# Attention, ELU-MoE and SoLU-MoE: a planned opening, v in halves, and four weight fetches moved behind the last stores

## The chip, the cores and the metric

One core of one Trainium2 chip runs the whole program once. The metric is device time in microseconds. Engines are TensorE (PE; PEld is its weight load), VectorE (DVE), ScalarE (ACT), GpSimd (POOL) and SyncE (SP), which issues the DMAs.

## What is computed

Three blocks in a row, on 4608 tokens of 512 features. Inputs are fp32; the weights come to the chip as 64-bit words.

```
k_p, v_p = k, v averaged over groups of 8 positions            # 576 -> 72
a = exp(s - max s),  s = q k_p^T / 8;  a = a / (sum a + 1e-9)
x = a v_p                                                       # 8 batches x 8 heads
h = x w_in;  g = h if h > 0 else exp(h) - 1;  x = g w_out       # 512 -> 2048 -> 512
h = x w2_in; e = exp(h - max h);  u = h * e / (sum e + 1e-9)    # 512 -> 1024
y = ((u - mean u) / sqrt(var u + 1e-6) * g_ln) w2_out           # -> 512
```

## The kernel before

**Work and stages.** Attention is cut into 32 units: 8 batches of NP = 4 head pairs. A unit loads k, q and v (`att_load`), sums k and v over groups of 8 (`att_kr`, `att_vr`), scales the sums (`att_kc` by 1/64, `att_vc` by 1/8, both on ACT), multiplies q with k (`att_scores`), takes maximum, exponential and normaliser (`att_max`, `att_exp`, `att_soft`), transposes on PE (`att_T`), multiplies with v (`att_V`) and splits the result into a high and a low fp32r part, `xh` and `xl` (`att_x`). Every large product is three products of such parts: high by high, low by high, high by low.

The ELU-MoE goes over blocks of 512 tokens. The first three blocks are done plainly, an h tile at a time (`h` L893, `o` L948). The other six go as three pairs, by a scheme of seven products instead of eight (`h_step` L1088, `mul_o` L1178). Attention units of later blocks are laid between. Weights are converted on chip from the 64-bit words (`conv`, L685 to L695: ACT, then DVE) and split into parts (`conv_split`, L709 and L710: ACT, then POOL).

The SoLU-MoE follows, again with seven products, over pairs n of token tiles. Product by product it writes the banks X, Y and Z (`z_mul`, PE L1285): P1 writes X, P2 writes Y, S2 adds onto X, and so on. ACT copies X to an `sn` tile after P1 and after S2 (`snap`, L1295), before the next product may add to it. From X, Y, Z and the copies come two tiles, `ha` and `hb`. Each goes through maximum, `e` (L1342), product with the normaliser (DVE L1348), subtraction of the mean (ACT L1353) and squares (L1358). Then the tile is turned: a few on PE (`pt`, L1404, copied by ACT L1410), the others by DVE in 32x32 squares (L1372), stored to memory (`zd`, L1377), loaded again (`dT`, four DMAs, L1384) and split by ACT (`dhl<-dT`, L1392) and DVE. The last product is `po` (L1423), 24 matmuls; ACT scales it into `ot` (L1429), which is stored.

**Who sets the order.** Each engine runs its instructions in program order. Three things set it.

- The opening (loads and `startup()`, L1466 to L1612) stands inside `tc.manual_schedule()` and runs as written. `busy(n, tag)` there puts n small matmuls without use on PE, in five calls of 6, 3, 8, 4 and 7. Being fp32, each of them shows as two rows in the trace and as one in the listings of order below.
- What is recorded up to the end of the ELU-MoE is ordered by `settle` (L31 to L270): it lists the instructions with assumed costs and due times, runs through them in assumed time and takes on each engine what is ready and most urgent.
- The SoLU-MoE is ordered by `arrange` (from about L1825). Each step is an entry `op(key, eng, dur, deps, f, ..., lat, at)`: its engine, assumed duration, what it waits for, and an assumed latency behind it. PE's order is fixed by the list `seq`; the other engines' order follows from assumed times.

Before the SoLU-MoE its weights are brought in by `fetch` (L799). The last four, `(0, 0)` to `(1, 1)`, are the parts of w2_out (`w<-o2d`, 1 MB each), which `po` needs. They are called at the end of the last pair, ahead of `p2_load(1)` (`x1r<-x1d`, L1228) and of the last two stores `x1d<-xo` (`o_done`, L1192). `arrange` knows nothing of them:

```python
deps = [("lo2", n)] + ([("st", outs[j - 2])] if j > 1 else [])
op(k, "PE", 5.46, deps + [before], z_out, n)
...
op(("hi2", i), "ACT", 1.0, [("l", i)] + free3, t_hi, i)
op(("p1", n), "ACT", 0.56, [("P1", n), ("ha0", n - 1)], snap, n, "p1", "X")
```

`hi2` is the row `dhl<-dT`, `("l", i)` its load, `p1` the first `sn` copy of pair n.

Of the kernel before, what the change touches and what calls it, by code (L numbers as in the profile page):

```python
# [22 lines left out]
class Step:  # L23
    def __init__(self, eng, idx, key):
        self.eng, self.idx, self.key = eng, idx, key
        self.ins, self.acc, self.deps, self.tiles, self.turn = [], [], set(), [], set()
        self.dur = self.lat = 0.0
        self.bytes = 0


def settle(tc, nc, stacks, PEND=2.6, WINDOW=10):  # L31
    GAP, RATE, LOOK = 0.06, 350e3, 0.35
# [32 lines left out]
    def cost(op, i, ins, outs):  # L65
# [9 lines left out]
        n = max(cols(o) for o in ins + outs)  # L75
        if op.eng == "SP":
            op.dur += 0.37
            op.bytes += max(o.ap[0][1] * cols(o) * size(o) for o in (ins[0], outs[0]))
        elif op.eng == "DVE":
            op.dur, op.lat = max(0.18, 0.068 + n * (0.0013 if str(outs[0].dtype).endswith("uint32") else 0.00109)), 0.09  # L80
        elif op.eng == "Activation":
            op.dur, op.lat = max(0.28, (0.057 if type(i).__name__ == "InstActivation" else 0.026) + n * 0.00096), 0.1
        else:
            op.dur, op.lat = 0.1 + n * 0.003, 0.1

    ops, fixed = [], 0
    for i in list(nc.cur_bb.bb.instructions):
# [5 lines left out]
        eng = str(i.engine).split(".")[-1]  # L93
        ins, outs = ([o for o in x if hasattr(o, "bass_ap")] for x in (i.ins, i.outs))
        fi, fo = [foot(o) for o in ins], [foot(o) for o in outs]
        key = fo[0][0] if fo else None
        if not (eng == "PE" and ops and ops[-1].eng == "PE" and ops[-1].key == key and len(ops[-1].ins) < 12):
            ops.append(Step(eng, len(ops), key))
        op = ops[-1]
        op.ins.append(i)  # L100
# [91 lines left out]
    for o in ops:  # L192
        if o.eng == "PE":
            want[o] = t
            t += o.dur
    latest = {}
    for o in reversed(topo):
        lat = PEND + 0.1 + o.bytes / RATE if o.eng == "SP" else o.lat
# [4 lines left out]
    manual = {e: [o for o in ops[:fixed] if o.eng == e] for e in engines}  # L203
    chain = [o for o in ops[fixed:] if o.eng == "PE"]
    ready = {e: {} for e in engines + (None,)}
    for o in ops:
        if not left[o]:
            ready[o.eng][o] = 0.0
    free, done, begun, order = dict.fromkeys(engines, 0.0), {}, {}, {e: [] for e in engines}
    lag = pipe = 0.0  # L210
    for _ in ops:
        best = min(((x, None, o) for o, x in ready[None].items()), key=lambda x: x[0], default=None)
        for e in engines if best is None else ():
            r, f = ready[e], free[e]
            if not r:
                continue
            if manual[e]:
                k = manual[e][0]
                if k not in r:
                    continue  # L220
            elif e == "PE":
                chain = [o for o in chain if o not in done] if chain and chain[0] in done else chain
                near = [o for o in chain[:3 * WINDOW] if o not in done][:WINDOW]
                near = [o for o in near if o in r]
                if not near:
                    continue
                first = min(max(f, r[o]) for o in near)
                k = next(o for o in near if max(f, r[o]) <= first + 0.02)
            else:
                first = min(max(f, x) for x in r.values())  # L230
                k = min((o for o in r if r[o] <= first + LOOK), key=lambda o: latest[o] + 3.0 * max(0.0, r[o] - first))
                for q in r if e in ("Activation", "DVE") else ():
                    end = max(f, r[k]) + k.dur
                    if q is not k and r[q] < end:
                        mine = max(0.0, end - latest[q] - lag)
                        other = max(0.0, max(f, r[q]) + q.dur - latest[k] - lag)
                        if other < mine - 0.05:
                            k = q
            begin = max(f, r[k])
            if best is None or begin < best[0]:  # L240
                best = begin, e, k
        begin, e, k = best
        if e == "PE":
            lag = max(lag, begin - want[k])
        begun[k] = begin
        if e is not None:
            free[e] = begin + k.dur
        if e is None:
            done[k] = begin
        elif e == "SP":  # L250
            pipe = max(free[e] + PEND - 0.8, pipe) + k.bytes / RATE
            done[k] = pipe + 0.9
        else:
            done[k] = free[e] + k.lat
        if e is not None:
            order[e].append(k)
            if manual[e]:
                manual[e].pop(0)
        del ready[e][k]
        for q in after[k]:  # L260
            left[q] -= 1
            if not left[q]:
                ready[q.eng][q] = max(
                    [done[d] + (0 if d.eng == q.eng == "PE" else GAP) for d in q.deps] + [begun[d] for d in q.turn]
                )
# [8 lines left out]
def kernel(  # L274
# [68 lines left out]
    NTREE = 3  # L343

# [13 lines left out]
    def att_load(i, what="kqv"):  # L358
        b, p = units[i]
        if i < NP:  # L360
            if ("kq", p) not in st:
# [3 lines left out]
                n = P * POOL  # L365
                v_t = st["v2"][0:SK, (p % 2) * n:(p % 2 + 1) * n].rearrange("s (c t) -> s c t", t=POOL)
                st["kq", p] = (kq[:, 0:S], kq[:, S:2 * S], v_t)
            k_t, q_t, v_t = st["kq", p]
        else:
            k_t = pa.tile([P, S], F32, name=f"k{i}", tag="k", bufs=1)  # L370
            v_t = pa.tile([SK, P, POOL], F32, name=f"v{i}", tag="v", bufs=1)
# [8 lines left out]
        if "v" in what:  # L380
            nc.sync.dma_start(out=v_t, in_=v[b, p].rearrange("s h d t -> s (h d) t"))

    def pool_tree(dst, src):
        n = POOL // 2
        while n > 1:
            nc.gpsimd.tensor_tensor(src[:, :, 0:n], src[:, :, 0:n], src[:, :, n:2 * n], op=ALU.add)
            n //= 2
        nc.gpsimd.tensor_tensor(dst, src[:, :, 0], src[:, :, 1], op=ALU.add)
# [25 lines left out]
    def att_kc(i):  # L414
        kp, kr = att_kv(i)[0], st.pop(("kr", i))
        nc.scalar.mul(kp[0:64, 0:SK], kr[0:64, :], 1.0 / (8 * POOL))
        nc.scalar.mul(kp[64:128, SK:2 * SK], kr[64:128, :], 1.0 / (8 * POOL))

    def att_vr(i):
        v_t = st["kq", units[i][1]][2] if i < NP else st["ld", i][1]  # L420
        vr = st["vr", i] = pa.tile([SK, P], F32, name=f"vr{i}", tag="vr")
        if i < NTREE:
            pool_tree(vr, v_t)
        else:
            nc.vector.tensor_reduce(vr, v_t, axis=AX, op=ALU.add)

    def att_vc(i):
        nc.scalar.mul(att_kv(i)[1], st.pop(("vr", i)), 1.0 / POOL)

    def att_setup(i):  # L430
        for part in (att_kr, att_kc, att_vr, att_vc):
            part(i)
# [50 lines left out]
    def att_soft(i):  # L483
# [82 lines left out]
    def rest(part):  # L566
# [15 lines left out]
        elif part == 1:  # L582
# [3 lines left out]
            nc.vector.tensor_scalar(sm, sm, 1e-9, None, op0=ALU.add)  # L586
# [68 lines left out]
    def conv_load(key):  # L655
# [1386 lines left out]
```

## Time and profile before

| what | value |
|---|---|
| median of 3 runs | 1245.41 us (1244.01 to 1245.87) |
| the profiled execution | 1244.96 us |
| its span in the profile | 1243.2 us, so 1.76 us lie around it |
| mean granted clock of TensorE | 0.998 |
| PE, DVE, ACT, POOL busy | 99%, 80%, 67%, 14% |
| chain that ended last | PE 95%, DVE 3%, DMA 1% |
| DMA | 263.31 MB, mean 212 GB/s |

The span runs from the first instruction to the last. A busy share is an average over stages of different kinds: the opening, in which PE waits for loads and for DVE, and the rest, where PE streams. A timeline row gives start, duration, engine, line and operation, and in brackets how long the engine had been idle before it and what ended that. Matmul rows overlap; 512-column matmuls of one stream start 0.23 us apart.

### The profile page before, as it was taken

The page shows a single profiled execution, that of the slowest core. Times are in us where ns is not written, and L with a number is a line of the kernel's source. Part 1 is how long each engine was busy: PE and PEld are TensorE (multiplying, and loading weights), DVE is VectorE, ACT ScalarE, POOL GpSimd, SP SyncE. Part 2 cuts the span into 40 slices and gives each one's busy share as a digit, 9 for nine tenths or more (in the row PEclk, how much of TensorE's full clock was granted, in tenths as well). Part 3 has the DMA queues.
Part 4 walks back from the last instruction along what each step waited for, and adds up shares of the span by engine and source line. Part 5 has one row for each costly group of instructions (what it writes and reads, how often), then busy time and mean ns, then how long its engine had stood idle before and what let it go on. Part 6 is the DMA issues. An engine that isn't in the chain of part 4 may idle for free.

```text
span 1243.2 us, 17288 instructions
## 1 busy us (share of the span) xinstructions
PE 1229.9 (99%) x5768; PEld 993.1 (80%) x5768; DVE 995.0 (80%) x1484; ACT 827.1 (67%) x1405; POOL 170.4 (14%) x148
## 2 busy tenths in 40 slices
PE   7999999999999999999999999999999999999998
PEld 6777787777787878788888788888888888888887
DVE  8898999898677789875788587997788787878763
ACT  7789666666657785557774477753676776767664
POOL 4645222332210011000000000000000000000000
PEclk9999999999999999999999999999999999999999
DMA  9598667677456867796667888788545544554341
GB/s 317 171 283 260 215 223 245 223 263 262 142 177 209 249 211 237 223 309 200 205 202 223 280 272 272 248 264 323 208 156 170 161 131 158 167 156 144 110 151 53
DMA packets 177065, 263.31 MB, mean 212 GB/s; under 512 B 16464, under 2 KB 96848, under 8 KB 175952
## 3 DMA queue, kind: packets, MB, share of 16 engines
q1 hardware_dynamic: 176976, 262.21, 65.6%
q8 instruction: 46, 0.75, 0.2%
q14 instruction: 43, 0.35, 0.1%
HBM read 182.46 MB, written 79.69 MB: 211 GB/s over the span
## 4 chain that ended last, share of the span: by engine, by line
PE 95%; DVE 3%; DMA 1%; issue 1%; ACT 0%; SPq 0%; ACTq 0%; DVEq 0%
PE po L1423 16%; PE hA L1088 16%; PE oA L1178 16%; PE o L948 10%; PE h L893 10%; PE zX L1285 8%; PE zZ L1285 4%; PE at L446 3%; PE oB L1178 3%; PE hB L1088 3%; PE at L531 3%; PE zY L1285 2%; PE pt L505 2%; PE pr L510 0%; DVE es L495 0%
## 5 line engine op out<-in xcount | busy, mean ns | idle before, releaser
L1423 PE MATMUL po<-w,dhl 128*128 128x512 f32 x864 | 203.7, 392 | 0.0
L1178 PE MATMUL oA<-op,wr 128*128 128x512 f32 x864 | 202.3, 392 | 0.0
L1178 PEld LDWEIGHTS oA<-op,wr 128*128 128x128 f32 x864 | 160.9, 188 | 37.6 <-issue 2.2
L1423 PEld LDWEIGHTS po<-w,dhl 128*128 128x128 f32 x864 | 162.1, 188 | 35.2
L1168 ACT CAST op<-g 128x1024 fp32r<-128x1024 f32 x84 | 87.7, 1052 | 59.7 <-PE oA L1178 34.8
L1169 DVE TENSOR_TENSOR op<-g,op 128x1024 fp32r<-128x1024 f32 x84 | 102.7, 1230 | 21.0 <-ACT op L1168 20.3
L1088 PE MATMUL hA<-sS,wr 128*128 128x512 f32 x414 | 104.0, 393 | 0.1
L1285 PE MATMUL zX<-w,xh 128*128 128x512 f32 x288 | 100.8, 392 | 0.0
L1363 POOL TENSOR_TENSOR sc<-sc,mhalf 128x1 f32<-128x1 f32 x36 | 20.9, 585 | 559.2 <-DVE sc L1362 295.3
L814 POOL TENSOR_TENSOR wol<-wo,woh 128x512 fp32r<-128x512 f32 x48 | 70.0, 1458 | 161.8 <-ACT woh L813 161.7
L1088 PEld LDWEIGHTS hA<-sS,wr 128*128 128x128 f32 x414 | 76.8, 188 | 18.7 <-issue 1.4
L495 POOL TENSOR_TENSOR es<-es,sm 128x720 f32<-128x720 f32 x28 | 43.5, 1552 | 312.2 <-DVE sm L493 228.8
L893 PE MATMUL h<-xh,wh 128*128 128x512 f32 x192 | 78.3, 408 | 1.4 <-DVE e L910 1.4
L948 PE MATMUL o<-gh,woh 128*128 128x512 f32 x192 | 78.2, 407 | 0.0
L893 PE MATMUL h<-xh,wl 128*128 128x512 f32 x192 | 75.2, 392 | 0.0
L893 PE MATMUL h<-xl,wh 128*128 128x512 f32 x192 | 75.2, 391 | 0.0
L948 PE MATMUL o<-gh,wol 128*128 128x512 f32 x192 | 75.0, 391 | 0.0
L1100 ACT COPY sp<-hA 128x512 f32<-128x512 f32 x72 | 42.3, 588 | 40.3 <-PE hA L1088 39.3
L1108 DVE SCALAR_TENSOR_TENSOR g<-ep,g 128x512 f32<-128x512 f32 x72 | 50.5, 703 | 20.9 <-ACT ep L1107 20.6
L1285 PEld LDWEIGHTS zX<-w,xh 128*128 128x128 f32 x288 | 54.1, 188 | 12.3
L1295 ACT COPY sn<-zX 128x512 f32<-128x512 f32 x54 | 31.8, 588 | 47.2 <-PE zX L1285 47.0
L1162 DVE TENSOR_TENSOR g<-g,g 128x1024 f32<-128x1024 f32 x48 | 61.0, 1288 | 0.1
(366 smaller groups left out, 2755.0 us busy)
## 6 DMA issues: line engine op xcount, KB each, us to landing
wr<-w3d SPq DMA_DIRECT2D x168, 256.0 KB, 2.8
wr<-w1d SPq DMA_DIRECT2D x161, 256.0 KB, 3.1
raw<-in_w SPq DMA_DIRECT2D x48, 512.0 KB, 6.8
dT<-zd SPq DMA_DIRECT2D x128, 128.0 KB, 2.7
v<-in_v SPq DMA_DIRECT2D x32, 288.0 KB
x1r<-x1d SPq DMA_DIRECT2D x9, 1024.0 KB, 5.9
out<-ot SPq DMA_DIRECT2D x36, 256.0 KB, 3.0
w1d<-ci SPq DMA_DIRECT2D x16, 512.0 KB, 3.3
```

The source lines that it names most:

```text
L495: eng.tensor_tensor(es, es, bc(sm, n), op=ALU.mult)
L814: nc.gpsimd.tensor_tensor(ol, t[:, f % 4, :], oh.bitcast(F32), op=ALU.subtract)
L893: nc.tensor.matmul(h[:, 0:n], a[g][:, kk, fo:fo + P], x[j][:, kk, 0:n], start=(kk == 0 and m == 0), stop=(kk == KDM - 1 and m == 2), skip_ ...
L948: nc.tensor.matmul(acc, a[:, dm * P:(dm + 1) * P], x[:, 0:n], start=(f == 0 and m == 0), stop=(f == NF - 1 and m == 2))
L1088: nc.tensor.matmul(bank, w[:, a, kk], x[:, b, kk], start=(start and m == 0), stop=(stop and m == 5), skip_group_check=True,)
L1108: gate["dve"] = nc.vector.scalar_tensor_tensor(d, e, 1.0, h, op0=ALU.subtract, op1=ALU.max).ins
L1162: nc.vector.tensor_tensor(d, x, y, op=op)
L1168: gate["act"] = nc.scalar.copy(o[:, 0], src).ins
L1169: gate["dve"] = nc.vector.tensor_tensor(o[:, 1], src, o[:, 0].bitcast(F32), op=ALU.subtract).ins
L1178: nc.tensor.matmul(banks[d], ws[i][:, a, d * P:(d + 1) * P], o[:, b, i], start=(start and t == 0 and i == 0 and m == 0), stop=(stop and t ...
L1285: nc.tensor.matmul(bank, x[:, o:o + P], w[:, y + k, :], start=(start and m == 0), stop=(stop and m == 5), skip_group_check=True,)
L1423: nc.tensor.matmul(po, a[:, c], b[c // 4][:, c % 4, :], start=(m == 0), stop=(m == 3 * NC2 - 1))
```

## The change

It does eight things.

1. `settle` gets other assumed costs: issue times of SP, a model of 16 DMA pipes by packet size, a port that DVE and POOL share. It treats each `busy` matmul as a step of its own that it puts where it expects PE to be idle.
2. The opening is no longer manual: `settle` orders it, the first loads excepted. `busy(56, "B")` is one call of 56 instead of 28 in five.
3. k's scaling in units 1 to 3 (`KPOOL`), and the normaliser product in units 2 and 3 (`NPOOL`), go to POOL.
4. v is laid out as two halves of 64 columns; `att_vc` is gone, and its 1/8 is folded into the normaliser, which is multiplied by 8.
5. The 64-bit words of w_in come as one 1 MB transfer, not as two of 512 KB. The first two conversions work in halves, through a PSUM tile `cu`.
6. The loads of i4, o4, i6, unit 4 and the rest move from ahead of `startup()` into it.
7. For the last pair, the first o product is split in two and stands between the last h products (`o_step`).
8. The four fetches move out of the last pair into `arrange`, as SP steps that form a chain; each `po` waits for the last of them. So they come behind the last `x1d<-xo` stores.

```diff
+    def idle(key):
+        return key is not None and key.startswith("busy")
...
+                    if fill is not None and at(fill) + (0.28 if f > 6.0 else 0.55) < first:
+                        k = fill
+                        k.dur = 0.26 if f > 6.0 else 0.52
...
     def att_kc(i):
         kp, kr = att_kv(i)[0], st.pop(("kr", i))
+        if i in KPOOL:
+            nc.gpsimd.tensor_scalar(kp[0:64, 0:SK], kr[0:64, :], 1.0 / (8 * POOL), None, op0=ALU.mult)
+            nc.gpsimd.tensor_scalar(kp[64:128, SK:2 * SK], kr[64:128, :], 1.0 / (8 * POOL), None, op0=ALU.mult)
+            return
...
-    def att_vc(i):
-        nc.scalar.mul(att_kv(i)[1], st.pop(("vr", i)), 1.0 / POOL)
...
-        nc.vector.tensor_scalar(sm, sm, 1e-9, None, op0=ALU.add)
+        nc.vector.tensor_scalar(sm, sm, 1e-9, float(POOL), op0=ALU.add, op1=ALU.mult)
         nc.vector.reciprocal(sm, sm)
-        eng = nc.vector if i < NP else nc.gpsimd
+        eng = nc.vector if i < NP and i not in NPOOL else nc.gpsimd
...
-        for a in range(2):
-            c, d = i + a, raw[:, a, :]
-            if kind == "i":
-                nc.sync.dma_start(
-                    out=d.rearrange("p (k f) -> p k f", k=KDM),
-                    in_=w_in[:, c * P:(c + 1) * P].rearrange("(k p) f -> p k f", p=P),
-                )
...
+        if kind == "i":
+            nc.sync.dma_start(
+                out=raw.rearrange("p a f -> p (a f)").rearrange("p (k f) -> p k f", k=KDM),
+                in_=w_in[:, i * P:(i + 2) * P].rearrange("(k p) f -> p k f", p=P),
+            )
...
+        busy(56, "B")
         att_kr(0)
         att_kc(0)
-        busy(6, "B")
         S_(0)
...
-    with tc.manual_schedule():
+    with ExitStack():
         for i in range(NP):
             att_load(i, "kq")
...
             if last and s == 6:
-                for n in ((0, 0), (0, 1), (1, 0), (1, 1)):
-                    fetch(n)
                 p2_load(1)
                 with loose(gate["x1r"]):
                     o_done(c, s)
...
     op("x1", None, 0.0, [], at=17.0)
+    for m, n in enumerate(((0, 0), (0, 1), (1, 0), (1, 1))):
+        op(("o2", n), "SP", 0.5, [("o2", p) for p in ((0, 0), (0, 1), (1, 0))[max(m - 1, 0):m]], fetch, n, lat=9.0)
...
-            deps = [("lo2", n)] + ([("st", outs[j - 2])] if j > 1 else [])
+            deps = [("lo2", n), ("o2", (1, 1))] + ([("st", outs[j - 2])] if j > 1 else [])
             op(k, "PE", 5.46, deps + [before], z_out, n)
```

**How instructions move: PE in the opening.** Around the last attention product ahead of the first h tile (`at<-a,kz`, the fourth of its kind), before:

```order
L531 MATMUL at_341<-a_288,kz 64x512 x2
L1493 MATMUL busy<-ident 128x128 x4
L505 MATMUL pt_0_356<-ident,es_265 72x128 x4
L505 MATMUL pt_1_362<-ident,es_265 72x128 x4
L531 MATMUL at_368<-a_312,kz 64x512 x2
L1493 MATMUL busy<-ident 128x128 x7
L531 MATMUL at_384<-a_355,kz 64x512 x2
L893 MATMUL h_398<-xh_325,wh 128x512
```

and with the change:

```order
L559 MATMUL pt_1_339<-ident,es_226 72x128 x4
L1561 MATMUL busy<-ident 128x128 x8
L585 MATMUL at_379<-a_310,kz 64x512 x2
L559 MATMUL pt_0_387<-ident,es_284 72x128 x4
L559 MATMUL pt_1_393<-ident,es_284 72x128 x4
L585 MATMUL at_399<-a_332,kz 64x512 x2
L1561 MATMUL busy<-ident 128x128
L585 MATMUL at_406<-a_386,kz 64x512 x2
L1561 MATMUL busy<-ident 128x128
L961 MATMUL h_420<-xh_128,wh 128x512
```

Of the seven fills ahead of the last product one is left there, one stands behind it, and eight stand ahead of the second product, where four stood. Further on, six fills stand ahead of the fourth slice of the first h tile and seven ahead of the second tile.

**ACT at the first `po`.** Pair 2 begins behind the first `po`. `sn<-zX` are its copies, `dhl<-pt` belongs to a tile turned on PE, `dhl<-dT` to one turned through memory. Before:

```order
L1295 COPY sn<-zX 128x512
L1353 ACTIVATE e_8696<-e_8696,sc 128x1024
L1295 COPY sn<-zX 128x512
L1410 CAST dhl<-pt_8735 128x512
L1410 CAST dhl<-pt_8740 128x512
L1358 ACTIVATE sq,sc<-e_8689 128x1024
L1295 COPY sn<-zX 128x512
L1342 ACTIVATE e_8805,sc<-ha,sc 128x1024
L1429 ACTIVATE ot<-po,sc 128x512
L1358 ACTIVATE sq,sc<-e_8696 128x1024
L1353 ACTIVATE e_8805<-e_8805,sc 128x1024
L1392 CAST dhl<-dT 128x1024
```

and with the change:

```order
L1426 ACTIVATE sq,sc<-e_8623 128x1024
L1426 ACTIVATE sq,sc<-e_8630 128x1024
L1330 CAST xh_8615<-x1r_8449 128x512
L1330 CAST xh_8615<-x1r_8449 128x256
L1330 CAST xh_8615<-xs_8659 128x1024
L1460 CAST dhl<-dT 128x1024
L1497 ACTIVATE ot<-po,sc 128x512
L1363 COPY sn<-zX 128x512 x2
L1478 CAST dhl<-pt_8734 128x512
L1478 CAST dhl<-pt_8739 128x512
L1410 ACTIVATE e_8756,sc<-ha,sc 128x1024
L1363 COPY sn<-zX 128x512
```

`dhl<-dT` and the first `ot` have moved from behind three `sn` copies to ahead of the first two of them. PE's order at this place is the same in both: `po`, then P1 (zX), P2 (zY) and S2 (zX) of pair 2.

**SP at the end of the last pair**, before:

```order
L1192 DMA x1d<-xo 128x512 x2
L806 DMA w_8488<-o2d 128x2048
L806 DMA w_8490<-o2d 128x2048
L806 DMA w_8492<-o2d 128x2048
L806 DMA w_8494<-o2d 128x2048
L1228 DMA x1r_8496<-x1d 128x4x512
L1192 DMA x1d<-xo 128x512 x2
L1228 DMA x1r_8683<-x1d 128x4x512
L1377 DMA zd_81<-hb 128x4x256
```

and with the change:

```order
L1260 DMA x1d<-xo 128x512 x2
L1296 DMA x1r_8449<-x1d 128x4x512
L1260 DMA x1d<-xo 128x512 x2
L874 DMA w_8471<-o2d 128x2048
L874 DMA w_8531<-o2d 128x2048
L874 DMA w_8609<-o2d 128x2048
L1296 DMA x1r_8617<-x1d 128x4x512
L874 DMA w_8647<-o2d 128x2048
L1445 DMA zd_81<-hb 128x4x256
L1452 DMA dT<-zd_81 32x4x256 x4
```

The four `w<-o2d` have moved behind the last two `x1d<-xo` and the first `x1r`, and the last of them behind the second `x1r`.

## Rows read from the trace of the kernel before

**Rows 1.** The page: each engine's busy time, share of the span, instructions.
```profile
PE 1229.9 (99%) x5768; PEld 993.1 (80%) x5768; DVE 995.0 (80%) x1484; ACT 827.1 (67%) x1405; POOL 170.4 (14%) x148
```

**Rows 2.** Waits of PE, whole program: waiter, releaser, us, times, longest.
```profile
PE pt L505 <- DVE es L495: 2.9, 2, 1.9
...
PE rs L572 <- PE at L446: 0.7, 1, 0.7
...
PE at L531 <- ACT kz L428: 0.2, 1, 0.2
```

**Rows 3.** Timeline of PE, 0 to 40: start us, us, instruction, [idle before].
```profile
11.39 1.95 PE L1493 MATMUL busy<-ident 128*128 128x128 f32 x16
...
27.70 3.07 PE L1493 MATMUL busy<-ident 128*128 128x128 f32 x14
30.70 1.08 PE L531 MATMUL at<-a,kz 72*64 72x512 f32 x4
...
38.84 0.50 PE L893 MATMUL h<-xh,wh 128*128 128x512 f32 x1 [1.39 <-DVE e L910]
```

**Rows 4.** Timeline of ACT, 10 to 40.
```profile
28.59 0.31 ACT L428 ACTIVATE kz<-vr 72x128 f32<-72x128 f32 x1
```

**Rows 5.** Stretches: busy us per engine (x count), granted clock, DMA share, GB/s.
```profile
10.00:24.00 14.00, 11.02 (x78) 7.89 (x76) 13.10 (x24) 13.91 (x50) 9.42 (x10) 1.00 1.06 332
28.00:32.00 4.00, 4.00 (x19) 3.07 (x19) 3.97 (x5) 2.65 (x7) 1.21 (x1) 0.71 1.07 347
860.00:884.00 24.00, 24.00 (x110) 19.70 (x109) 13.23 (x21) 10.86 (x19) 0.00 (x0) 1.00 0.97 375
884.00:1239.00 355.00, 355.00 (x1562) 290.82 (x1560) 269.59 (x476) 240.00 (x362) 20.86 (x36) 1.00 0.44 139
```

**Rows 6.** Timeline of PE, 876 to 912.
```profile
884.15 5.66 PE L1423 MATMUL po<-w,dhl 128*128 128x512 f32 x24
...
892.43 0.39 PE L1285 MATMUL zX<-w,xh 128*128 128x512 f32 x1
```

**Rows 7.** Timeline of ACT, 876 to 906.
```profile
891.24 0.59 ACT L1295 COPY sn<-zX 128x512 f32<-128x512 f32 x1 [1.04 <-PE zX L1285]
891.72 1.15 ACT L1353 ACTIVATE e<-e,sc 128x1024 f32<-128x1024 f32 x1
...
899.30 0.68 ACT L1429 ACTIVATE ot<-po,sc 128x512 f32<-128x512 f32 x1
...
902.40 1.04 ACT L1392 CAST dhl<-dT 128x1024 fp32r<-128x1024 f32 x1
```

**Rows 8.** Instructions of L495: count, ns min/median/max, first and last start us.
```profile
L495 POOL TENSOR_TENSOR es<-es,sm x28: 1392/1394/2450, 59.1 to 646.3; 128x720 f32<-128x720 f32 x28
...
L495 DVE TENSOR_TENSOR es<-es,sm x4: 808/1274/1814, 13.3 to 23.4; 128x576 f32<-128x576 f32 x4
```

**Rows 9.** Timeline of SP, 855 to 912: DMA issues.
```profile
861.78 3.14 SPq L806 DMA_DIRECT2D w<-o2d  x4
...
876.29 0.53 SPq L1228 DMA_DIRECT2D x1r<-x1d  x1
894.58 0.38 SPq L1377 DMA_DIRECT2D zd<-hb  x1
897.50 1.76 SPq L1384 DMA_DIRECT2D dT<-zd  x4
```

**Rows 10.** Timeline of DVE, 876 to 912.
```profile
883.61 1.22 DVE L1336 TENSOR_REDUCE sc<-hb 128x1 f32<-128x1024 f32 x1 [0.44 <-ACT hb L1326]
...
889.30 1.28 DVE L1348 SCALAR_TENSOR_TENSOR e<-e,sc,hb 128x1024 f32<-128x1024 f32 x1
...
890.70 1.22 DVE L1266 TENSOR_TENSOR xl<-xs,xh 128x1024 fp32r<-128x1024 f32 x1
...
893.31 1.24 DVE L1372 STREAM_TRANSPOSE hb<-e 128x1024 f32<-128x1024 f32 x1
```

**Rows 11.** The tile dT: landing times of its loads.
```profile
DMA to landing us min/median/max: 2.2/2.7/4.0
```

More of the change, by code (lines that the diff above doesn't have):

```diff
@@ L27, in __init__, with settle @@
         self.dur = self.lat = 0.0
-        self.bytes = 0
-def settle(tc, nc, stacks, PEND=2.6, WINDOW=10):
-    GAP, RATE, LOOK = 0.06, 350e3, 0.35
+        self.bytes = self.move = self.wide = 0
+        self.port = False
+def settle(tc, nc, stacks, PEND=2.6, FAST=1.7, WINDOW=10):
+    GAP, LOOK = 0.06, 0.35
     masks = {}
@@ L194, in settle @@
             want[o] = t
-            t += o.dur
+            t += o.dur * (not idle(o.key))
     latest = {}
     for o in reversed(topo):
-        lat = PEND + 0.1 + o.bytes / RATE if o.eng == "SP" else o.lat
+        lat = PEND + 0.1 + o.move if o.eng == "SP" else o.lat
         lat += o.dur + (GAP if o.eng not in ("PE", None) else 0)
@@ L202, in settle @@
     engines = ("PE", "Activation", "DVE", "Pool", "SP")
[L203 to L219, printed above, removed]
-                    continue
[L221 to L228, printed above, removed]
-            else:
[L230 to L264, printed above, removed]
-                )
@@ L266, in settle @@
+    order, begun, done = forward(latest)
     info = mybir.DependencyInfo(mybir.DependencyClass.NoSync, mybir.DependencyReason.DATA)
@@ L380, in att_load @@
         if "v" in what:
[L381 removed]
+            nc.sync.dma_start(out=v_t, in_=v[b, p])
     def pool_tree(dst, src):
@@ L683, in conv @@
         wcv[key] = w2
+        if key in (("i",0),("o",0)):
+            for a in range(2):
+                c = slice(512 * a, 512 * a + 512)
+                u = ps.tile([P, 512], F32, name="cu", tag="A", bufs=4)
+                t = u.bitcast(U32)
+                nc.scalar.activation(u, hw.bitcast(F32)[:, c], AF.Abs, scale=2.0**-112)
+                nc.scalar.activation(lw[:, c], raw.bitcast(U8)[:, 3::8][:, c], AF.Identity, scale=1.0 / 32, bias=b31)
+                if a:
+                    yield
+                nc.vector.scalar_tensor_tensor(t, t, 3, lw[:, c], op0=ALU.logical_shift_left, op1=ALU.bitwise_or)
+                nc.vector.scalar_tensor_tensor(
+                    wu[:, c], hw[:, c], 0x80000000, t, op0=ALU.bitwise_and, op1=ALU.bitwise_or
+                )
+            yield
+            return
         nc.scalar.activation(w, hw.bitcast(F32), AF.Abs, scale=2.0**-112)
@@ L1509, in startup @@
         att_kc(2)
-        busy(3, "B")
         S_(2)
@@ L1518, in startup @@
         att_kc(3)
-        busy(8, "B")
         T(0)
@@ L1538, in startup @@
         att_x(0)
+        for key in (("i", 4), ("o", 4), ("i", 6)):
+            conv_load(key)
+        att_load(NP)
+        rest_load()
         att_vr(3)
@@ L1752, with o_step @@
         count = 0
+        def o_step(s, t, ds=(0, 1)):
+            nonlocal step, credit
+            if t == ds[0] == 0:
+                ox["b"] = o_banks(s, "CBA" if last else "ABA")
+            banks = ox["b"]
+            mul_o(s, t, banks, s in (0, 1, 2), s in (1, 5, 6), ds)
+            if ds[-1] == 0:
+                return
+            if s + 1 < 7:
+                for i in range(2):
+                    w_ring(("o", s + 1, 2 * t + i))
+                n = ORDER[s + 1]
+                if n in ("S2", "S3"):
+                    g_sum(n, t)
+                if n == "S4":
+                    with loose(gate["dve"]):
+                        g_sum(n, t)
+                with loose(gate["keep"]) if last and s == 4 else ExitStack():
+                    g_op(s + 1, t)
+            elif not last:
+                for m in (2 * t, 2 * t + 1):
+                    if m < 7:
+                        w_ring(("i", 0, m))
+                sx_next(c + 2, t + 2)
+            if s == 5 and not last and t in (0, 3):
+                sx_next(c + 2, t // 3)
+            if s < 5:
+                credit += 2 * rate
+                while credit > 0.999 and step < aim:
+                    att_half(step)
+                    step += 1
+                    credit -= 1.0
+            for _ in range(LATE.get((s, t), 0) if last else 0):
+                late.pop(0)()
+            if last and (s, t) == (6, 1):
+                p2_split(1)
         for i in range(NFP + 1):
```

215 lines of the change are left out of this document (142 added, 73 removed).

## The prediction

> **What bounds the kernel now.** I read the page first, then TensorE's waits, then the timelines of the first 40 us, then the place where the last phase takes over (860 to 910 us), since the diff touches both ends.
>
> The page: PE is busy 1229.9 of 1243.2 us [rows 1], so all its idle time is 13.3 us. Whatever the change saves must come out of those 13.3 us or out of PE work that computes nothing; whatever wait it adds on PE is lost in full. The view of PE's waits has eight entries that sum to 9.2 us, from the 2.9 for `es` down to 0.2, nearly all of it in the opening [rows 2].
>
> PE's rows show where. From 27.70 on, 7 fills run (14 rows, two for each), and behind them the last attention product, at 30.70 [rows 3]. That product was ready earlier: its last operand, the ACT scaling of v, ended at 28.59 + 0.31 = 28.90 [rows 4]. So 1.80 us go to fills that the written order put in front of it. Next, PE stands 1.39 us before the third h tile, which starts at 38.84 [rows 3], and 0.7 ahead of `rs` [rows 2]. In the stretch 28 to 32 the granted clock is 0.71, against 1.00 from 10 to 24 [rows 5]: part of it ran at 1.2 instead of 2.4 GHz, after PE had stood for the longest of its waits, the 1.9 us for `es` [rows 2]. The 7 fills there took 3.07 us, 0.44 each; the 8 at 11.39, 16 rows, took 1.95, 0.24 each [rows 3]. The loads bound the opening as well: from 10 to 24 and from 28 to 32 no DMA engine is free, at 332 and 347 GB/s [rows 5]. So it can't shrink by all that PE waits.
>
> At the other end PE is busy 24.00 of 24 us before 884 and all of the 355 us from there to 1239 [rows 5]. Here the first `po` begins at 884.15; behind it run P1 and P2 of pair 2, and at 892.43 S2, which adds onto P1's bank [rows 6]. Before it adds, ACT must have copied that bank into `sn`: 891.24 + 0.59 = 891.83 [rows 7], 0.6 us of margin.
>
> **The change, part by part.** *Opening.* Gone are 28 ACT scalings of v outside the opening, beside PE's stream and worth nothing, and four in it; the factor 8 rides in a DVE instruction that is there already. The last of the four stood directly in front of the product at 30.70 and belongs to the 1.80 us. Single w_in loads move the same bytes in fewer issues on DMA engines without free room: nothing, and the bounds below hold what there may be. The planner now places each of 56 fills where it expects PE to idle, instead of 28 where they were written. By the listing one fill stands ahead of the last product instead of 7, so I book the 1.80. The third h tile comes behind more work, so the 1.39 goes; the `rs` wait, 0.7, goes where the plan spreads the pieces. Together 3.9. Against it stand 13 fills now inside the first h tiles (six and seven): at 0.24 us they cost 3.2 if the plan's holes aren't real and 0 if they are. I take half, 1.6. **The opening gains 3.9 - 1.6 = 2.3 us.** Late next is the last `xl` slice, which the first h tile needs before it can end. Bounds: nothing gained (holes missed, POOL late), or 5, if the fills cost nothing and 1.1 of the 2.9 us for `es` goes too; DVE, busy 13.10 of the 14 us from 10 to 24 [rows 5], hardly allows more.
>
> The normaliser product of units 2 and 3 goes to POOL. DVE is rid of two rows between 0.81 and 1.81; the nearest POOL rows are those with 720 columns, 1.39 to 2.45, median 1.394 [rows 8], at 576 columns an estimate of 1.1. That is 0.3 more than DVE's shortest and less than its longest, and I book nothing. The Trainium skill, page GPSIMD Engine Reference, section "Engine selection", speaks against the move: elementwise work with two inputs belongs on VectorE, as GPSIMD is about twice as slow. The rows here give 1.1 to 0.81, not two to one. By the rule the products would take an estimated 1.6, some 0.5 more for each of the two transposes behind them, and the sum below would rise by 1.0 at most.
>
> *The k scalings on POOL and the first conversions in halves* lie in the opening and in its bounds. *The first o product, split around the last h products,* moves PE work within a stretch that DVE and ACT feed ahead; I book nothing, and its price is in rival C.
>
> *The four fetches, and what they do to ACT's order.* This is the large term. The fetches now come after the last xo stores and are steps of the last phase's planner. Their entries form a chain: each waits for the one before, four times 0.5 + 9.0, 38 us, and every `po` waits for the last. The chip issued all four within 3.14 us [rows 9]. So the plan holds the first `po` until 38, while by its own PE durations (twelve products of 1.365, one transposition of 0.87) that `po` would come at some 17.3. Into these 20 us, which it believes free, it puts ACT's work for other tiles, what must come back from memory among it. The listing shows it: `dhl<-dT` and then `ot` stand ahead of both `sn` copies of pair 2, where before they stood behind three of them. PE's own order there is the same: `po`, P1, P2, S2. The chip follows the plan's order, not its times: `po` runs when its weights are there.
>
> So PE runs `po`, P1, P2, and stands at S2 until ACT has done, in this order: the wait for dT, `dhl`, `ot`, `sn`. In times of the trace of before: DVE's transposition of that tile needs ACT's subtraction (1.15 us; before it began at 891.72, behind an `sn` [rows 7]; now it can follow DVE's product, which ended at 889.30 + 1.28 = 890.58) and stands behind DVE's `xl`, which ended at 890.70 + 1.22 = 891.92 [rows 10]. It starts at 891.95 and, with 1.24, ends at 893.2; before, it ended at 893.31 + 1.24 = 894.55. Then comes the trip through memory: zd issued at 894.58, the last of four dT loads at 897.50 + 1.76 - 0.42 = 898.84 [rows 9], landing a median 2.7 us after its issue [rows 11], at 901.54: 6.96 us. From 893.2 it ends at 900.15. `dhl` takes 1.04, `ot` 0.68, `sn` 0.59 [rows 7], less 0.1 of overlap at each of two joints: 902.25. S2 stood at 892.43. **The stall is 9.8 us**, and nothing gives it back, for PE has no idle time behind it.
>
> Bounds: from below the bare chain of that tile, with no queueing at all. Its maximum ends at 883.61 + 1.22 = 884.83; then come the exponential and the subtraction, 1.15 each, between them the product with its small rows, 1.8, then the transposition 1.24, the trip 6.96, and 2.1 for `dhl`, `ot` and `sn`: 899.2, so 6.8 us [rows 7, 10, 11]. From above, dT landing 4.0 instead of 2.7 after issue [rows 11]: 11.1. I take 9.8, which is nearest to the rows as they queue.
>
> The fourth fetch now stands on SP behind an x1r load whose issue waited until 876.29 for PE [rows 9]. Two transfers of 1 MB, at the 375 GB/s of that stretch [rows 5], are 5.6 us, so it lands near 883; its words are needed half a `po` after 884.15, at 886.9. Were it 2 us too late, `po` would be 2 us later and the stall 2 us shorter, for dT doesn't wait for `po`: nothing in the sum.
>
> **Sum**, against the profiled execution's own 1244.96 us (1.76 around its span; 0.45 below the median of the runs, 1245.41): 1244.96 - 2.3 + 9.8 = **1252.5 us**.
>
> **Rivals.** *A, the tile is back in time (faster).* If S2 of pair 2 doesn't wait for dT, only the opening's gain is left: 1244.96 - 2.3 = 1242.7. It is faster only if the stall is all but gone, under 0.2 us, or the opening gains more. For it speaks that ACT is lightly loaded from 860 to 884, 10.86 of 24 us [rows 5], and could reach the tile's work sooner; against it, that even the bare chain leaves 6.8. Chance 0.08.
>
> *B, the opening gains nothing.* The fills sit where there is no hole, or PE stands and the granted clock falls as it did at 28 to 32, and the stall stays: 1244.96 + 9.8 = 1254.8. For it: the plan's costs are fitted numbers, and its belief about the last phase shows what such numbers can do. Against it: the 7 fills are gone from the place where they cost 1.80. Chance 0.12.
>
> *C, the middle gains waits.* The planner's costs changed for every engine, and pieces were moved between PE blocks. Four new waits as long as that of `rs`, 0.7 each, make 2.8 us: 1255.3. Against it: outside the opening PE's waits hold no entry of 1 us [rows 2]. Chance 0.08.
>
> **How the numbers follow.** The forecast has the remaining 0.72, with its own range from 1244.96 - 5 + 6.8 = 1246.8 to 1244.96 + 11.1 = 1256.1. B and C lie inside it. The range given is 1247 to 1257; it leaves out A and little else. A measurement of this kernel can tell about 0.2%, 2.5 us, from no change: faster is below 1242.9, slower above 1247.9. Faster: A, 0.08. The same: the forecast with both terms at their good ends, or a stall of a few us, 0.08. Slower: the rest, 0.84.
>
> **What would show it.** In the profile after: one idle of about 10 us on PE between P2 and S2 of pair 2, behind the first `po`, ended by ACT's `sn`, and ACT idle ahead of `dhl<-dT` until the dT load lands; no other new PE wait over 1 us; the third h tile some 2 us before 38.84, and no stretch at the lower clock around 28 us. If PE streams through the first two `po`, I misread the order and A holds. If the stall is there and the total near 1255, the opening failed.

## The result, and the profile after

The changed kernel takes 1252.77 us (median of 7 runs, 1251.32 to 1258.59), the kernel before 1245.87 beside it. The ratio is 1.006, 95% interval 1.0042 to 1.0078: slower, by about 7 us. The forecast was 1252.5.

The profiled execution of the changed kernel took 1258.59 us, 5.8 more than the median; where that lies is the first question of the experiments. The page of that execution, with PE's busy time and the chain that ended last, answers to [rows 1]:

```profile
span 1256.8 us, 17365 instructions
...
PE 1236.9 (98%) x5824; PEld 1001.5 (80%) x5824; DVE 979.0 (78%) x1485; ACT 822.4 (65%) x1372; POOL 178.8 (14%) x156
...
PE 96%; DMA 2%; ACT 1%; DVE 1%; issue 0%; SPq 0%; ACTq 0%
```

PE's busy time rose by 7 us though it has no product more to do; part of it are 28 more fills, part matmuls at the lower clock. The view of PE's waits (waiter, releaser, us, times, longest) answers to [rows 2]. The waits for `es`, for DVE's `e` and for `rs` are gone; those for the identity, for the copies `a` and for kz (now from POOL) are left, and the first is new:

```profile
PE zX L1353 <- ACT sn L1363: 9.9, 1, 9.9
PE pt L559 <- ACT a L560: 2.6, 1, 2.6
PE at L500 <- POOL kz L471: 1.6, 2, 1.0
PE busy L1561 <- POOL ident masks.py:199: 1.4, 1, 1.4
```

The new wait stands where it was forecast. PE's timeline, with P2's last matmul and the first of S2 of pair 2, answers to [rows 6]:

```profile
892.86 0.40 PE L1353 MATMUL zY<-w,xh 128*128 128x512 f32 x1
903.14 0.79 PE L1353 MATMUL zX<-w,xh 128*128 128x512 f32 x1 [9.88 <-ACT sn L1363]
903.73 0.63 PE L1353 MATMUL zX<-w,xl 128*128 128x512 f32 x1
904.16 1.05 PE L1353 MATMUL zX<-w,xh 128*128 128x512 f32 x2
```

ACT's timeline beside it, to [rows 7]: ACT waits 2.64 us for the dT load, then does `dhl`, `ot` and `sn`, in this order, and S2 begins when `sn` is done.

```profile
897.29 1.04 ACT L1330 CAST xh<-xs 128x1024 fp32r<-128x1024 f32 x1 [1.63 <-DVE xs L1325]
900.98 1.04 ACT L1460 CAST dhl<-dT 128x1024 fp32r<-128x1024 f32 x1 [2.64 <-DMA dT<-zd]
901.93 0.68 ACT L1497 ACTIVATE ot<-po,sc 128x512 f32<-128x512 f32 x1
902.51 0.57 ACT L1363 COPY sn<-zX 128x512 f32<-128x512 f32 x1
```

SP's timeline, to [rows 9]. The three fetches are issued behind the last stores, the fourth behind the second x1r, and still no `po` waits for weights. The trip of the tile runs from zd at 893.93 to `dhl` at 900.98, 7.05 us:

```profile
866.90 2.28 SPq L874 DMA_DIRECT2D w<-o2d  x3
876.95 0.53 SPq L1296 DMA_DIRECT2D x1r<-x1d  x1
877.52 0.63 SPq L874 DMA_DIRECT2D w<-o2d  x1
893.93 0.37 SPq L1445 DMA_DIRECT2D zd<-hb  x1
896.85 1.75 SPq L1452 DMA_DIRECT2D dT<-zd  x4
```

What the forecast did not have is behind the stall. The view of stretches (busy per engine, granted clock, DMA share, GB/s) gives a clock of 1.00 before it and 0.50 just after it, and the matmuls of S2 start 0.43 us apart (903.73 to 904.16) instead of 0.23. PE is back at full clock at about 908.7. In the opening of this execution there is such a stretch too, at 24 to 28.

```profile
24.00:28.00 4.00, 3.93 (x21) 3.82 (x22) 3.67 (x8) 4.00 (x8) 1.84 (x3) 0.57 0.94 366
890.00:892.90 2.90, 2.90 (x15) 2.29 (x13) 2.78 (x5) 2.27 (x3) 0.00 (x0) 1.00 0.00 0
...
902.90:907.00 4.10, 3.86 (x12) 3.17 (x13) 0.98 (x2) 0.82 (x3) 0.00 (x0) 0.50 0.31 115
```

An overlay compares the start of each matmul with that of the same matmul in the profiled execution of before. By it the changed kernel is 0.66 us late when pair 2 begins, and 13.33 late from S2 to the end. So the place costs 12.67 us: 9.88 of idle, the rest at the lower clock.

### The profile page after: what moved, and what is told of

It is laid out like the page before. It is cut to its first block, busy times and chain, and to the rows that moved or that the text cites. A ratio compares the mean times of both kernels' runs of the same rounds, so it can differ in the third digit from the quotient of the medians.

```text
span 1256.8 us, 17365 instructions
## 1 busy us (share of the span) xinstructions
PE 1236.9 (98%) x5824; PEld 1001.5 (80%) x5824; DVE 979.0 (78%) x1485; ACT 822.4 (65%) x1372; POOL 178.8 (14%) x156
## 4 chain that ended last, share of the span: by engine, by line
PE 96%; DMA 2%; ACT 1%; DVE 1%; issue 0%; SPq 0%; ACTq 0%
PE hA L1156 16%; PE po L1491 15%; PE oA L1246 12%; PE h L961 11%; PE o L1016 11%; PE zX L1353 8%; PE zZ L1353 4%; PE oC L1246 3%; PE at L585 3%; PE at L500 3%; PE hB L1156 3%; PE oB L1246 3%; PE pt L559 2%; PE zY L1353 2%; DMA raw<-in_w 1%; PE busy L1561 1%
## 5 line engine op out<-in xcount | busy, mean ns | idle before, releaser
L1246 PE MATMUL oA<-op,wr 128*128 128x512 f32 x672 | 158.2, 392 | 0.0
L1246 PEld LDWEIGHTS oA<-op,wr 128*128 128x128 f32 x672 | 125.1, 188 | 30.1 <-issue 2.9
L882 POOL TENSOR_TENSOR wol<-wo,woh 128x512 fp32r<-128x512 f32 x48 | 76.4, 1596 | 134.7 <-ACT woh L881 134.7
L549 POOL TENSOR_TENSOR es<-es,sm 128x720 f32<-128x720 f32 (+1 forms) x30 | 48.2, 1607 | 326.2 <-DVE sm L547 229.8
L971 ACT ACTIVATE e<-h 128x512 f32<-128x512 f32 x48 | 28.6, 597 | 48.5 <-PE h L961 48.4
```

Source lines behind the costliest of these rows:

```text
L549: eng.tensor_tensor(es, es, bc(sm, n), op=ALU.mult)
L882: nc.gpsimd.tensor_tensor(ol, t[:, f % 4, :], oh.bitcast(F32), op=ALU.subtract)
L1246: nc.tensor.matmul(banks[d], ws[i][:, a, d * P:(d + 1) * P], o[:, b, i], start=(start and t == 0 and i == 0 and m == 0), stop=(stop and t ...
```

## The experiments

Each ratio is to the kernel before, run on the same chip beside it, with its 95% interval. Times are medians.

**1. A second profile of the change.** No edit.

> The changed kernel once more, for a second profile, because its profiled execution took 1258.59 us and its other six between 1251.32 and 1253.63. Theory (the 5.8 us lie in the opening, where ACT stood 3.99 us for the first w_in words in the profiled execution): an execution near 1252.5 has the same idle of 9.9 us ahead of S2 of pair 2 and the same lower granted clock behind it, while the third h tile, at 42.03 in the first profile, starts at about 36.5. Rival (the 5.8 us lie in the middle or at the end): the third h tile starts at about 42 again in an execution near 1252.5.

1251.14 us. The wait of PE for `sn` is the same:

```profile
PE zX L1353 <- ACT sn L1363: 9.7, 1, 9.7
```

The opening is not. In the first profile ACT waits 3.99 us for the first w_in words, whose conversion its order has ahead of the copies for the next transposes; in the second it waits 0.43. ACT's timelines, of the first and of the second profile:

```profile
20.36 1.20 ACT L743 ACTIVATE cu<-raw 128x512 f32<-128x512 f32 x2 [3.99 <-DMA raw<-in_w]
```

```profile
15.85 1.21 ACT L743 ACTIVATE cu<-raw 128x512 f32<-128x512 f32 x2 [0.43 <-DMA raw<-in_w]
```

The transposes that wait for these copies then start late in the first profile, and the last V product begins at 31.89 (PE's timeline), against 25.80 in the second:

```profile
24.07 1.46 PE L559 MATMUL pt<-ident,es 128*72 128x128 f32 x8 [2.56 <-ACT a L560]
...
31.89 1.08 PE L585 MATMUL at<-a,kz 72*64 72x512 f32 x4
```

The third h tile starts at 42.03 in the first profile and at 35.86 in the second; before, at 38.84 [rows 3]. When the last phase begins, the change is 0.66 us behind before in the one and 5.72 ahead in the other. The two executions are 7.45 us apart: 6.2 of it lie in the opening, where both run the same instructions in the same order, and 1.05 at the stall, which costs 11.62 us in the second instead of 12.67. So the 5.8 us lie in the opening, and the usual opening gains more than forecast.

**2. The fetches back in the last pair.**

```diff
             if last and s == 6:
+                for n in ((0, 0), (0, 1), (1, 0), (1, 1)):
+                    fetch(n)
                 p2_load(1)
...
-    for m, n in enumerate(((0, 0), (0, 1), (1, 0), (1, 1))):
-        op(("o2", n), "SP", 0.5, ...)
...
-            deps = [("lo2", n), ("o2", (1, 1))] + ...
+            deps = [("lo2", n)] + ...
```

> The change without its eighth part: the four fetches are called in the last pair as before, and po waits for nothing more in the plan. Theory (the plan's 38 us set ACT's order, and that order costs 9.9 us of idle and 2.7 us at the lower clock): sn stands ahead of dhl<-dT again, no wait over 1 us behind the first po, and the time falls by some 12.5 us to about 1240.2, 5 under before. Rival (the wait comes from the replanned middle or from transfers that compete there): some 1252, as with the whole change.

1242.17 us, ratio 0.9971 (0.996 to 0.9982). The stall is gone, and the kernel is faster than before. This profile has a later wait for `sn`, 1.4 us near 954, which that of run 12 has too (1.3) and no other in more than 0.2 us.

**3. The fetches where the change has them, without the chain.**

```diff
-        op(("o2", n), "SP", 0.5, [("o2", p) for p in (...)[max(m - 1, 0):m]], fetch, n, lat=9.0)
+        op(("o2", n), "SP", 0.5, [], fetch, n, lat=9.0)
```

> The change with the four fetches where it puts them, behind the last stores, and with po still waiting for the last of them in the plan; but they don't wait for one another, so that the plan has po free at 11 us instead of 38. Theory (what counts is the plan's belief, not the place of the fetches): the order of ACT is that of before, and the time is that of the run without the eighth part, about 1240.2, within 1.5 us. Rival (the fetches come late on the chip, behind the last stores, and po or the x1r loads wait for them): po waits for its weights, and the time stays within 3 us of the whole change, near 1250 to 1252.

1240.80 us, ratio 0.9959 (0.9947 to 0.9972). This is the test that tells the two theories apart: the four fetches are issued behind the last stores, the first three as in the change (the fourth no longer behind the second x1r), and `po` waits for nothing. All of PE's waits:

```profile
PE busy L1561 <- POOL ident masks.py:199: 1.4, 1, 1.4
PE pt L559 <- ACT a L560: 0.6, 1, 0.6
PE at L500 <- POOL kz L471: 0.2, 1, 0.2
PE zX L1353 <- ACT sn L1363: 0.2, 1, 0.2
```

ACT's timeline has the first `sn` ahead of `ot` and `dhl` again:

```profile
886.29 0.59 ACT L1363 COPY sn<-zX 128x512 f32<-128x512 f32 x1 [1.04 <-PE zX L1353]
...
894.36 0.68 ACT L1497 ACTIVATE ot<-po,sc 128x512 f32<-128x512 f32 x1
...
897.46 1.03 ACT L1460 CAST dhl<-dT 128x1024 fp32r<-128x1024 f32 x1
```

So fetching behind the last stores costs nothing, and the plan's belief costs the 12 us.

**4. The eighth part alone, on the kernel before.** The opposite edit of run 2, made in the kernel before.

> The kernel before with the eighth part alone: the fetches as a chain in the last phase's planner. Theory: the same stall of 9.9 us and the same 2.7 us at the lower clock, nothing else changed: 1245.9 + 12.6 = 1258.5. Rival (the stall needs the replanned opening and middle as well): within 3 us of before.

1257.50 us, ratio 1.0093 (1.008 to 1.0107), some 12 us above before. By the overlay the place costs 11.55 us here. The stall needs nothing else of the change; the opening's waits are of the same kinds as before:

```profile
PE zX L1285 <- ACT sn L1295: 9.9, 1, 9.9
PE pt L505 <- DVE es L495: 3.5, 2, 2.0
PE h L893 <- DVE e L910: 2.4, 1, 2.4
```

**5. Fills in the stall.** In the changed kernel, ahead of S2 of pair 2:

```diff
+        if (n, key) == (2, "S2"):
+            t = ps.tile([P, 512], F32, name="busy", tag="C")
+            for _ in range(36):
+                nc.tensor.matmul(t[:, 0:P], ident, ident, start=True, stop=True)
```

> The whole change, with 36 matmuls without use on PE between P2 and S2 of pair 2: some 8.7 us of the 9.9 that PE stands there. They change no order on ACT. Theory (the stall has two prices, 9.9 us of idle and 2 to 3 us of lower granted clock behind it, and the second comes from PE standing): the wait for sn shrinks to 1 or 2 us, S2 begins when it did, the granted clock behind it is 1.00, and the time falls by 2 to 2.5 us from the change's 1252.5 to about 1250.2. Rival (the slow matmuls behind the stall have another cause, such as operands that come late): S2 and the products behind it are as slow as they were, and the time stays at 1252.5 or rises.

1250.80 us, ratio 1.0043 (1.0029 to 1.0058). PE works off the fills and waits 2.01 us, and from the second matmul of S2 on they start 0.23 us apart, at a granted clock of 1.00:

```profile
887.45 8.20 PE L1383 MATMUL busy<-ident 128*128 128x128 f32 x72
897.66 0.50 PE L1353 MATMUL zX<-w,xh 128*128 128x512 f32 x1 [2.01 <-ACT sn L1363]
898.00 0.39 PE L1353 MATMUL zX<-w,xl 128*128 128x512 f32 x1
898.23 0.63 PE L1353 MATMUL zX<-w,xh 128*128 128x512 f32 x2
```

S2 still begins only when `sn` is done, 10.2 us after the fills began, but nothing behind it is slow. This place now costs 10.35 us by the overlay with before, against 12.67, 11.62 and 11.55 in the three profiles with the stall. So the slow matmuls came from PE's standing, and they are worth 1.2 to 2.3 us. The medians (1252.77 and 1250.80) differ by as much, though their intervals overlap.

**6. The first w_in words loaded first** (on run 3).

```diff
+        conv_load(("i", 0))
         att_load(0, "v")
         att_load(1, "v")
-        conv_load(("i", 0))
```

> The run without the chain (1240.8), with the first w_in words loaded ahead of v of units 0 and 1 instead of behind them. Theory (what differs between executions of the new opening is when these words land, 15.8 to 20.3 us, because ACT's order has their conversion ahead of the copies that the transposes wait for): ACT doesn't wait for them, the times lie closer together, and the median falls by 0.5 to 2 us, to about 1239.5. Rival (v of unit 0, now 2 us later, becomes what the first product waits for): 1241 to 1243.

1240.38 us (1240.20 to 1241.76), ratio 0.9959 (0.9947 to 0.9971). No difference from run 3 can be told; the five runs lie within 1.6 us, where those of run 3 lie within 3.2. ACT no longer waits for these words. The planner has also moved seven fills: 50 stand ahead of the first h tile and six behind its start, where run 3 has 43 and 13.

**7. 28 fills instead of 56** (on run 3): `busy(28, "B")`.

> The run without the chain (1240.8), with 28 fills instead of 56. By the prediction's step, the 13 fills inside the first h tiles cost half of 3.2 us: then 1239.2. Rival (the plan's holes are real, so that the fills cost nothing, and without them PE stands and the granted clock falls as it did at 28 us in the kernel before): 1240.8 to 1242.5, with a stretch below full clock between 20 and 35 us.

1242.88 us, ratio 0.9985 (0.9971 to 0.9999): the rival, by an interval that only just touches that of run 3. The fills earn time, but not in every execution. Of the 12, from 1240.50 to 1249.06, the three with a mean granted clock of 1.000 take 1240.50 to 1241.72, as run 3 does; the four at 0.994 to 0.996 take 1246.57 or more. The profiled one, 1246.57, is of these: PE stands 1.2 us at 20 us, and then runs at the lower clock until 35. Stretches of this execution:

```profile
20.00:24.00 4.00, 2.76 (x13) 1.60 (x13) 3.75 (x8) 4.00 (x9) 3.83 (x6) 0.68 1.02 378
24.00:28.00 4.00, 4.00 (x15) 1.59 (x12) 3.01 (x4) 3.23 (x7) 1.28 (x1) 0.50 1.01 389
28.00:32.00 4.00, 4.00 (x11) 1.59 (x8) 0.69 (x1) 2.89 (x4) 1.29 (x1) 0.50 1.09 302
32.00:38.00 6.00, 6.00 (x21) 4.77 (x21) 4.25 (x5) 3.33 (x6) 1.29 (x1) 0.74 1.02 360
```

**8. The normaliser products of units 2 and 3 on DVE** (on run 3): `NPOOL = ()`.

> The run without the chain (1240.8), with the normaliser products of units 2 and 3 on DVE again. The prediction booked nothing for their move to POOL: within 1 us of 1240.8. By the rule that such work belongs on VectorE, up to 1 us faster, 1239.8. Rival (DVE was the engine that held the opening, and the move is where its gain comes from): 1242 to 1243.

1241.43 us, ratio 0.9969 (0.9957 to 0.9981), an interval that overlaps that of run 3. The move to POOL neither pays nor costs anything that these runs can tell; the planner's order of the opening changed with it, the fills as in run 6.

**9. The first o product in one piece** (on run 3).

```diff
-                w_ring(("o", 0, 7))
-                o_step(0, 0, (0,))
...
-                if (i, s) == (NFP, 4):
-                    o_step(0, 0, (1,))
...
+        w_ring(("o", 0, 7))
...
-            for t in range(s == 0, 4):
+            for t in range(4):
```

> The run without the chain (1240.8), with the first o product of the last pair in one piece again, behind the last h products. Between 670 and 790 us the changed kernels gain 0.9 us on the kernel before, in every profile. Theory (the split gives it): 1240.8 + 0.9 = 1241.7, and waits of some 0.2 us on PE at 710 to 725 as before. Rival (the planner's new order gives it): 1240.8, and the 0.9 are there all the same.

1242.78 us, ratio 0.9976 (0.9962 to 0.9991), with runs from 1240.14 to 1250.78. The median speaks for the theory, though its interval overlaps that of run 3 and 0.35 us of it lie outside the span (2.1 us around it in the profiled execution, 1.76 in that of before). The profile, of an execution of 1241.00, speaks for the rival: between 586 and 730 us it gains the same 0.9 us as run 3. So the 0.9 us don't need the split; whether it pays stays open. Nor are they all the new order's: runs 4 and 11, whose order there is that of before, gain 0.4 and 0.5 in this stretch on the one profiled execution of before.

**10. 72 fills** (on run 6): `busy(72, "B")`.

> The run with the first w_in words loaded first (1240.4), with 72 fills instead of 56; by the listing the 16 more all stand ahead of the second h tile, where the plan sees a hole of 22 fills. Theory (the plan's hole there isn't real, or shorter): PE works off the fills while the tile's operands are ready, and the time rises by up to 16 times 0.24, 3.9 us: 1241.5 to 1244.3. Rival (the hole is real): no change, 1240.4.

1245.21 us, ratio 0.9994 (0.9984 to 1.0003), 4.8 above run 6 by the medians and 4.4 by the ratios. All 22 fills run back to back ahead of the second h tile, 5.08 us on the path, and the third begins 3.5 us later than in run 6's profile:

```profile
32.61 5.08 PE L1561 MATMUL busy<-ident 128*128 128x128 f32 x44
37.44 0.48 PE L961 MATMUL h<-xh,wh 128*128 128x512 f32 x1
```

**11. The last seven fills behind the last product** (on the kernel before).

```diff
-        busy(7, "B")
         att_V(3, double("A"))
+        busy(7, "B")
```

> The kernel before with its last 7 fills behind the last attention product instead of ahead of it, nothing else. The prediction counted 1.80 us for these fills. Theory (the product was ready and the h tiles can follow it): the product starts at about 29, the first h tile 1 to 1.8 us earlier, and the time falls by as much, to 1244. Rival (the first h tile comes behind the same fills in any case, since they only change places with the product): the same time, 1245.5.

1247.46 us, ratio 1.0006 (0.9997 to 1.0015): no gain, as the rival has it. In the profile, of an execution of 1248.55, the last two products run one behind the other, and PE runs slow from 26 to 36 us, with a granted clock of 0.50 in the stretch 28 to 32:

```profile
28.21 3.68 PE L531 MATMUL at<-a,kz 72*64 72x512 f32 x8
31.82 3.36 PE L1493 MATMUL busy<-ident 128*128 128x128 f32 x14
34.83 0.77 PE L893 MATMUL h<-xh,wh 128*128 128x512 f32 x1
```

Two products, 8 rows, take 3.68 us there, and the first h tile begins at 34.83 instead of 31.71. The run doesn't settle what the fills cost: they only change places with the product and still stand ahead of the first h tile. It shows that drawing the product ahead of them gains nothing.

**12. 50 fills** (on run 6): `busy(50, "B")`, so that only the six fills ahead of the second h tile are gone.

> The run with the first w_in words loaded first (ratio 0.9959 to before), with 50 fills instead of 56: the six that stood ahead of the second h tile are gone, those ahead of the first one stay. Theory (fills earn their time only up to the first h matmul, by keeping PE from standing; behind it the plan's hole isn't real, as 16 more there cost some 4 us): 6 times 0.24, about 1.5 us less, ratio 0.9947, and no stretch below full clock. Rival (without them PE stands there for as long, or the clock falls): ratio 0.9959 or above.

1243.69 us, ratio 0.9981 (0.9972 to 0.999), above run 6. The rival's number, but not for its reason: the granted clock stays at 1.00 in all of the opening, and PE doesn't stand at the second tile. Its profile, of an execution of 1244.97, shows a wait of 2.1 us for `es` earlier on, where the order up to there is that of run 6. DVE's `es` of unit 1 took 2.78 us, and 0.74 in run 6. DVE and POOL of this run, then of run 6:

```profile
17.05 2.78 DVE L549 TENSOR_TENSOR es<-es,sm 128x576 f32<-128x576 f32 x1
```

```profile
16.82 1.28 POOL L439 TENSOR_TENSOR v<-v 72x512 f32<-72x512 f32 x1
18.05 1.16 POOL L549 TENSOR_TENSOR es<-es,sm 128x576 f32<-128x576 f32 x1
```

```profile
16.83 0.74 DVE L549 TENSOR_TENSOR es<-es,sm 128x576 f32<-128x576 f32 x1
```

```profile
16.92 1.78 POOL L439 TENSOR_TENSOR v<-v 72x512 f32<-72x512 f32 x1
```

In run 6 DVE begins 0.09 us before POOL's sum of v, and is done in 0.74. Here POOL's sum begins 0.23 us before DVE, and DVE ends only when that sum and POOL's own `es` behind it are done. Two more waits, 1.1 us for a copy `a` at 123 and 1.3 for `sn` near 954, make up most of the rest of what this profile is behind run 6's. The six fills themselves seem to be worth nothing either way: it is 1.6 us behind run 6's at the first h tile and as much at the second block, for the planner put other work in their place.

## Why the prediction was right

**The stall, 9.8 us forecast, 9.88 measured.** The step held piece by piece: the plan's 38 us put `dhl<-dT` and `ot` ahead of the `sn` copies; the tile's trip was taken as 6.96 us and came as 7.05; `po` waited for no fetch. Run 4 shows that the eighth part is enough for it, runs 2 and 3 that it goes when the plan's belief goes. This is shown by four kernels, not argued.

**"Nothing gives it back": true, and more was to pay.** The sum had the idle alone. After it, PE runs at a granted clock of 0.50 for more than 5 us. The overlay gives 12.67 us for the place in the first profile, 11.62 in the second and 11.55 in run 4's; with fills it gives 10.35. So the term was mis-sized by 1.8 to 2.9 us. The same had been in plain sight in the opening of the kernel before [rows 5], and was used there, but not carried to the stall.

**The opening, 2.3 us forecast, about 4 in the usual execution, and 0.9 more at 586 to 730.** Mis-sized the other way. That the sum came out within 0.3 us is luck, two wrong sizes that cancel: 1245.87 - 5 + 12 is 1252.9. By the overlay of run 3 with before, 2.2 us are gained by the third h tile, 3.65 by the start of the second block (the `rs` wait, 0.7, and others), 4.0 by 586 us and 4.9 by 730. The first h tile of before, then the first and the third of run 3 (PE's timelines):

```profile
31.71 0.50 PE L893 MATMUL h<-xh,wh 128*128 128x512 f32 x1
```

```profile
27.82 0.48 PE L961 MATMUL h<-xh,wh 128*128 128x512 f32 x1
...
36.63 0.39 PE L961 MATMUL h<-xh,wh 128*128 128x512 f32 x1
```

The forecast's 1.39 and 0.7 were there: both waits are gone from the view of PE's waits. What failed is the pair of steps on fills.

- *"So I book the 1.80"* has the right sign but the wrong reason. The first h tile begins 3.9 us earlier in run 3, although 43 fills stand ahead of it instead of 28. The gain comes from PE's waits: the idle times in its timeline up to there sum to 2.2 us instead of 6.5, and the granted clock, 0.50 from 28 to 30 us before, is 1.00 in those stretches. What the seven fills cost by themselves no run shows.
- *"Half, 1.6"* was too little. From the first to the third h tile run 3 needs 8.81 us and before 7.13: the 1.39 is gone, but the 13 fills run there for 3.1. Run 6, with six of them, needs 7.26.

Fewer fills in all are no gain either: with 28, run 7 is 2.1 us slower than run 3 by the medians, through the executions at a lower clock. The 0.9 us at 586 to 730 were in no step. Which of the parts 1 to 6 ends which wait was not separated, but for the normaliser product.

**The normaliser product on POOL, booked at nothing: right.** POOL takes 1.14 to 1.16 us for it in runs 6 and 12 (estimate: 1.1) and DVE 0.75 in run 8, 1.5 to one, and the times don't tell run 8 from run 3. The rule of the Trainium skill, page GPSIMD Engine Reference, section "Engine selection", about two to one, by which the sum would have been up to 1.0 higher, isn't borne out here.

**The fourth fetch, booked at nothing: right.** It was issued at 877.52, and no `po` waits.

**Rivals.** A would have been a kernel with no stall, and 1242.7; runs 2 and 3 are that kernel, at 1242.17 and 1240.80. B's opening did come, in one execution: the profiled one gains nothing there, through ACT's wait for the first words, and with the slow matmuls behind the stall it took 1258.59, not B's 1254.8. C didn't come.

The version to keep is run 3 or run 6: the change, without the chain. Both are 0.41% faster than before (0.9959, at the widest 0.9947 to 0.9972) and about 1% faster than the change.

## What to carry to other kernels

A planner's assumed time is an order on the chip: a dependency with too long a latency costs nothing where it is written and much where the planner fills the time that it thinks is free. So read, in the listing, what an in-order engine has to wait for ahead of the instruction that the bound engine needs. A long stall of TensorE is to be charged with the slower matmuls behind it. A fill pays where PE would stand, as in run 5, and costs nearly its full length where it would not, as in run 10.

## What the runs showed of the hardware that was not expected

- The lower clock behind a stall is paid even in a phase that streams: PE stood for 9.88 us, and the stretch 902.9 to 907 ran at 0.50, with S2's matmuls 0.43 us apart. In run 5, with PE at work for most of that time, they ran at 1.00. The wait of 2.0 us there did not bring the clock down; one of 1.2 that ended at 21.5 us, after several shorter ones, came ahead of a low stretch in run 7.
- One DVE instruction with two inputs, `es`, took 0.74 us in run 6's profile, where it began 0.09 us ahead of POOL's sum, and 2.78 in run 12's, where it began 0.23 behind it. The Trainium skill, page SBUF — State Buffer, section "Who interferes with whom", has this as an exclusive lock: the two share a pair of ports, and the one that comes second is fully blocked, not slowed. The rows of this pair agree, and show a loser that waits for two POOL instructions in a row. Here a shift of 0.3 us became 2 us.
- ACT, which waits for the first w_in words, begins on them at 15.85 us in one execution of the changed kernel and at 20.36 in the other. Why they land so far apart is not settled; the DMA share from 10 to 24 us is 1.05 in both.
